# A last loop taken in halves: one PSUM bank for each z tile, a new order of steps, and batch ends stored late on two queues

## The chip, the cores and the metric

The kernel runs on one core of a Trainium2 chip. The core has five engines: PE (TensorE, matmuls; its weight loads are listed as PEld), DVE (VectorE), ACT (ScalarE), POOL (GpSimd) and SP (SyncE, which here only issues transfers), and 16 DMA engines that move data between the chip's memory and the core's. The metric is the device time of one launch in microseconds (us); smaller is better. A profile covers one execution, and its span is a little shorter than the time of the launch.

## The reference, cut to what matters

Attention with a causal mask and a decay bias makes `x`; a spectral layer follows. It transforms `x` over time, multiplies its 64 lowest modes by complex matrices (one 512 x 512 pair for each mode), transforms back to `y`, and returns `u + relu(u @ w_ch)` with `u = x + y`.

```python
# attention, for each of 8 batches and 8 heads, S = 576, D = 64
scores = where(causal, -1e9, scale * q @ k.T + minimum(bias, 0.0))
x = softmax(scores) @ v                       # -> (8, 576, 512)

# spectral layer
X = np.fft.rfft(x, axis=1)                    # only modes 0..63 are used
Y[:, :64] = X[:, :64] * (w_r + 1j * w_i)      # for each mode a 512x512 product
y = np.fft.irfft(Y, n=S, axis=1)
u = x + y
return (u + np.maximum(u @ w_ch, 0.0)).astype(np.float32)
```

The output is 8 x 576 x 512 float32, 9.44 MB. The weights `w_r` and `w_i` are 134 MB and are read once.

## The kernel before

The attention runs over 32 "images" (4 groups of two heads by 8 batches). While it runs, the weights of the modes are streamed in by transfers that POOL issues; the products of the modes follow as the weights come. The transform over time of one image:

```python
def fft(n):
    g, b = divmod(n, B)
    ps = auxpool.tile([P, 2, 3 * HM], FP32, name="ft_ps", tag="aux")     # HM = 32
    for T in range(NT):                                                  # NT = 5
        for q_ in range(2):
            nc.tensor.matmul(
                ps[HP * q_ : HP * q_ + HP].rearrange("p h f -> p (h f)"),
                x_all[:nT, g, b, T, q_::2], Ff_sb[:nT, T, :],            # 192 columns
                start=(T == 0), stop=(T == NT - 1), tile_position=(0, HP * q_), ...)
    for h in range(2):
        for q_ in range(2):
            ...                                                          # view a of ps
            nc.vector.tensor_copy(out=xs[g % 2][HP * h : HP * h + HP, q_, :, h, :, b, :], in_=a)
```

The output is made in 18 "pairs", each two tiles of 128 rows by 512 columns. A pair is two neighbouring tiles of one batch, or, twice, the ends of four batches: 576 = 4 x 128 + 64, so a batch's last 64 rows fill half a tile, and the ends of four batches fill one pair. The ends stand at places 2 and 4 of the list:

```python
pairs = [((b, T), (b, T + 1)) for b in range(B) for T in range(0, NF, 2)]   # NF = 4
for i, b in ((2, 0), (4, B // 2)):
    pairs.insert(i, ((b, NF), (b + 2, NF)))
NPRE = 2
kept = list(range(NPRE, len(pairs)))
ways = dict(zip(kept, "evgvggeggsgsgsgs"))
```

For a pair, `z = x @ w_ch + y @ w_ch`. The part from `x` is made earlier and kept in the core's memory (`z1s`, pairs 2 to 17); the letters say how it comes back: `e`, as two fp16 digits multiplied by the identity on PE; `s`, copied by ACT into the PSUM tile of z; `v`, added by DVE; `g`, added by POOL after ACT has copied z out. In the last loop each pair goes through these steps:

```python
zpool = ctx.enter_context(tc.tile_pool(name="z_psum", bufs=2, space=PSUM))   # a tile is two banks

def relu(i):                       # step R, ACT
    rs[i] = result(i)
    if ways.get(i) == "g":
        nc.scalar.copy(out=rs[i], in_=zs[i])
        nc.gpsimd.tensor_tensor(out=rs[i], in0=rs[i], in1=z1s[i], op=ALU.add)
        return
    n = 1 if i in (0, last) else 2
    for x in range(0, 2, n):
        nc.scalar.activation(out=rs[i][:, x : x + n], in_=zs[i][:, x : x + n], func=ACTF.Relu)
    if i in x_pool: ...            # x_pool is empty

def kept_sum(i):                   # step K, DVE
    rs[i] = result(i)
    nc.vector.tensor_tensor(out=rs[i], in0=zs[i], in1=z1s[i], op=ALU.add)

def finish(i):                     # step F, DVE and a store
    n = 1 if i in (0, last) else 2
    for x in range(0, 2, n):
        o, u = rs[i][:, x : x + n, :], us[i][:, x : x + n, :]
        if ways.get(i) in ("v", "g"):
            nc.vector.scalar_tensor_tensor(out=o, in0=o, scalar=0.0, in1=u, op0=ALU.max, op1=ALU.add)
        else:
            nc.vector.tensor_tensor(out=o, in0=u, in1=o, op=ALU.add)
        if T < NF:
            nc.sync.dma_start(out=out[b, ...].rearrange("(x p) e -> p x e", p=P), in_=o)
    if T == NF:
        for r, bb, _ in parts(b, T):                                     # two stores of 64 partitions
            nc.sync.dma_start(out=out[bb : bb + 3 : 2, NF * P :, :].rearrange("x t e -> t x e"), in_=rs[i][r])

steps = {"S": seed, "E": digits, "Z": add_z, "R": relu, "K": kept_sum, "X": add_x, "U": add_u, "F": finish}
for step in (
    "R0 X1 F0 U1 R1 E2 F1 Z2 Z3 R2 X2 K3 U2 Z4 F2 X3 R4 Z5 U3 K5 Z6 X4 R6 U4 F3 Z7 E8 R7 F4 Z8 X5 R8 "
    "Z9 U5 R9 X6 F5 U6 Z10 S11 F6 X7 U7 R10 Z11 F7 X8 R11 U8 Z12 F8 X9 S13 U9 X10 R12 F9 Z13 U10 R13 "
    "Z14 F10 X11 U11 S15 F11 X12 R14 U12 Z15 F12 X13 R15 U13 Z16 F13 X14 R16 U14 X15 F14 S17 U15 F15 "
    "X16 U16 Z17 F16 X17 R17 U17 F17 "
).split():
    steps[step[0]](int(step[1:]))
```

`Z` multiplies `y @ w_ch` (kept in `yv`) back over time into z, `X` puts `x` into the PSUM tile u, `U` adds `y` to it. Two matmuls of 512 columns make one such step of a full pair. `yv` is filled by small transfers (`spread`); the last of them comes after the last weights.

Of the kernel before, what the change touches and what calls it, by code (L numbers as in the profile page):

```python
# [18 lines left out]
def kernel(  # L19
# [60 lines left out]
    G_np = G_np.reshape(P, SP).astype(np.float16)  # L80
# [24 lines left out]
    G_sb = gp.tile([P, SP], FP16, name="G_sb")  # L105
# [318 lines left out]
    def fft(n):  # L424
        if n < 0:
            return
        g, b = divmod(n, B)
        ps = auxpool.tile([P, 2, 3 * HM], FP32, name="ft_ps", tag="aux")
        for T in range(NT):
            nT = tails[T]  # L430
            for q_ in range(2):
                nc.tensor.matmul(  # L432
                    ps[HP * q_ : HP * q_ + HP].rearrange("p h f -> p (h f)"),
                    x_all[:nT, g, b, T, q_::2], Ff_sb[:nT, T, :],
                    start=(T == 0), stop=(T == NT - 1),
                    tile_position=(0, HP * q_), skip_group_check=True,
                )
        for h in range(2):
            for q_ in range(2):
                a = ps[HP * q_ : HP * q_ + HP, h, : 2 * HM].rearrange("p (r m) -> p r m", r=2)  # L440
                a = bass.AP(tensor=a.tensor, offset=a.offset, ap=[a.ap[0], [HM, 2]] + list(a.ap[1:]))
                nc.vector.tensor_copy(out=xs[g % 2][HP * h : HP * h + HP, q_, :, h, :, b, :], in_=a)  # L442
# [50 lines left out]
    for i, b in ((2, 0), (4, B // 2)):  # L493
        pairs.insert(i, ((b, NF), (b + 2, NF)))
# [4 lines left out]
    ways = dict(zip(kept, "evgvggeggsgsgsgs"))  # L499
# [85 lines left out]
    zpool = ctx.enter_context(tc.tile_pool(name="z_psum", bufs=2, space=PSUM))  # L585
# [33 lines left out]

    def x_times_wch(i, last):  # L620
        zs[i] = z = zpool.tile([P, 2, DM], FP32, name="z_ps", tag="z")
        for x in range(2):
            for dt in range(DT):
                nc.tensor.matmul(  # L624
                    z[:, x, :], xts[i][:, x, dt, :], wch_sb[:, dt, :],
                    start=(dt == 0), stop=(last and dt == DT - 1), skip_group_check=True,
                )

    def keep(i):
        x_times_wch(i, True)  # L630
        j = late.index(i)
        if j < len(places):
            t = places[j]
        else:
            t = wpool.tile([P, WM, DM], BF16, name="z1", tag="w").rearrange("p m e -> p (m e)")
        kept_place(i, t)
        keep_product(i, slice(0, 2), zs.pop(i))
# [72 lines left out]
    x_pool = ()  # L710
    GK = P - 2 * MC * NX

    def add_y(dst, i, which, rows=slice(0, P), start=False):

        for x, (b, T) in enumerate(pairs[i]):
            for r, bb, _ in parts(b, T):
                nc.tensor.matmul(
                    dst[x][r, :], G_sb[rows, bass.ds(T * P, r.stop - r.start)],
                    yv[rows, bb, which, :], start=start, stop=True, skip_group_check=True,
                    tile_position=(0, r.start),  # L720
                )

    def add_last(dst, i, yb, cols=slice(0, DM), c=NX - 1):

        for x, (b, T) in enumerate(pairs[i]):
            nc.tensor.matmul(
                dst[x][:, cols], Gx_sb[:, c, bass.ts(T, P)], yb[:, cols],
                start=False, stop=True, skip_group_check=True,
            )
# [31 lines left out]
    def relu(i):  # L761

        rs[i] = result(i)
        if ways.get(i) == "g":
            nc.scalar.copy(out=rs[i], in_=zs[i])
            nc.gpsimd.tensor_tensor(out=rs[i], in0=rs[i], in1=z1s[i], op=ALU.add)  # L766
            return
        n = 1 if i in (0, last) else 2
        for x in range(0, 2, n):
            nc.scalar.activation(out=rs[i][:, x : x + n], in_=zs[i][:, x : x + n], func=ACTF.Relu)  # L770
        if i in x_pool:
            b, T = pairs[i][0]
            r = rs[i].rearrange("p x (g d) -> p x g d", d=P)
            nc.gpsimd.tensor_tensor(
                out=r, in0=r, in1=x_all[:, :, b, T : T + 2, :].rearrange("p g t d -> p t g d"), op=ALU.add
            )

    def kept_sum(i):
        rs[i] = result(i)
        nc.vector.tensor_tensor(out=rs[i], in0=zs[i], in1=z1s[i], op=ALU.add)  # L780

    def finish(i):
        n = 1 if i in (0, last) else 2
        b, T = pairs[i][0]
        for x in range(0, 2, n):
            o, u = rs[i][:, x : x + n, :], us[i][:, x : x + n, :]
            if ways.get(i) in ("v", "g"):
                nc.vector.scalar_tensor_tensor(out=o, in0=o, scalar=0.0, in1=u, op0=ALU.max, op1=ALU.add)
            else:
                nc.vector.tensor_tensor(out=o, in0=u, in1=o, op=ALU.add)  # L790
            if T < NF:
                nc.sync.dma_start(
                    out=out[b, bass.ds((T + x) * P, n * P), :].rearrange("(x p) e -> p x e", p=P), in_=o
                )
        if T == NF:
            for r, bb, _ in parts(b, T):
                nc.sync.dma_start(
                    out=out[bb : bb + 3 : 2, NF * P :, :].rearrange("x t e -> t x e"), in_=rs[i][r]
                )

    def z_of(i):
        return [zs[i][:, x, :] for x in range(2)]
# [55 lines left out]
    for i in range(NPRE):  # L858
        for cols in halves:
# [3 lines left out]
    def start_z(i):  # L863
        zs[i] = zpool.tile([P, 2, DM], FP32, name="z_ps", tag="z")

    def seed(i):
        start_z(i)
        nc.scalar.copy(out=zs[i], in_=z1s[i])

    def digits(i):  # L870
        start_z(i)
        for x in range(2):
            for y in range(2):
                nc.tensor.matmul(
                    zs[i][:, x, :], ident16h, z1s[i][:, y, x, :],
                    start=(y == 0), stop=False, skip_group_check=True,
                )

    def add_z(i):
        if i not in zs:  # L880
            start_z(i)
        add_y(z_of(i), i, 1, start=ways[i] in ("v", "g"))

    def add_u(i):
# [4 lines left out]

    steps = {  # L890
        "S": seed, "E": digits, "Z": add_z, "R": relu, "K": kept_sum, "X": add_x, "U": add_u, "F": finish,
    }
    for step in (
        "R0 X1 F0 U1 R1 E2 F1 Z2 Z3 R2 X2 K3 U2 Z4 F2 X3 R4 Z5 U3 K5 Z6 X4 R6 U4 F3 Z7 E8 R7 F4 Z8 X5 R8 "
        "Z9 U5 R9 X6 F5 U6 Z10 S11 F6 X7 U7 R10 Z11 F7 X8 R11 U8 Z12 F8 X9 S13 U9 X10 R12 F9 Z13 U10 R13 "
        "Z14 F10 X11 U11 S15 F11 X12 R14 U12 Z15 F12 X13 R15 U13 Z16 F13 X14 R16 U14 X15 F14 S17 U15 F15 "
        "X16 U16 Z17 F16 X17 R17 U17 F17 "
    ).split():
        steps[step[0]](int(step[1:]))
# [30 lines left out]
```

## Time and profile before

| | |
|---|---|
| time, median of 3 runs | 447.0 us (446.7 to 447.36) |
| span of the profiled execution | 445.1 us |
| busy: PE | 337.8 us (76%) |
| busy: DVE | 254.2 us (57%) |
| busy: ACT | 221.3 us (50%) |
| busy: POOL | 243.0 us (55%) |
| moved by the 16 DMA engines | 93.25 MB, mean 210 GB/s |

The busy shares are averages over stages with different limits, so none of them names the bound by itself. The page also cuts the span into 40 slices, follows the chain of work that ended last, and lists groups of instructions with their mean duration and the idle time before them. The trace answers the same by stretch of time. [...] Times within the span are counted from its start; the last loop begins at about 412.6 us.

### The profile page before, as it was taken

What the parts mean: (1) busy time and instruction counts of PE and PEld (TensorE: products, weight loads), DVE (VectorE), ACT (ScalarE), POOL (GpSimd) and SP (SyncE); (2) the same over time, 40 slices, a digit from 0 to 9 for tenths busy, and PEclk for the clock granted to TensorE, in tenths of its full rate; (3) what the DMA queues carried; (4) which work ended last, traced back from release to release, by engine and by line L of the source; (5) the groups of instructions that cost most, each with busy time, mean ns of one, the idle gap of its engine ahead of it and who ended that gap; (6) DMA issues with size and microseconds to landing.
All of it is one profiled execution on the core that took longest, in us unless ns stands there. A gap on an engine that the chain in (4) does not pass through costs nothing.

```text
span 445.1 us, 10791 instructions
## 1 busy us (share of the span) xinstructions
PE 337.8 (76%) x4409; PEld 209.9 (47%) x4409; DVE 254.2 (57%) x574; ACT 221.3 (50%) x387; POOL 243.0 (55%) x375
## 2 busy tenths in 40 slices
PE   1688897994908599792487859399987997768994
PEld 1365565563605465561354535266654555433341
DVE  7766776672705466662274627157765454541785
ACT  1576786463605374672263625267650344320593
POOL 7766666555556666455565546465544443530393
PEclk9998999996967889987598969689997799979998
DMA  9999999999999999999999999999999999996598
GB/s 174 202 206 205 204 207 204 207 207 208 207 209 202 205 203 187 207 206 209 207 200 206 209 206 203 208 205 205 199 209 211 210 210 210 209 218 131 168 351 346
DMA packets 72672, 93.25 MB, mean 210 GB/s; under 512 B 29664, under 2 KB 31200, under 8 KB 72624
## 3 DMA queue, kind: packets, MB, share of 16 engines
q0 software_dynamic: 63408, 81.29, 104.3%
q1 hardware_dynamic: 9216, 11.29, 7.9%
q8 instruction: 34, 0.56, 0.5%
q14 instruction: 14, 0.11, 0.1%
HBM read 163.51 MB, written 9.44 MB: 389 GB/s over the span
## 4 chain that ended last, share of the span: by engine, by line
DMA 58%; PE 22%; POOL 6%; issue 5%; DVE 5%; ACT 2%; POOLq 1%; DVEq 0%; ACTq 0%
DMA qk<-in_k_dram 19%; DMA w_sb<-in_moe_w_i_dram 16%; DMA w_sb<-in_moe_w_r_dram 16%; PE yp L452 4%; PE z_ps L624 4%; PE sc_ps L378 3%; POOL r_w L766 3%; PE tr_ps L336 2%; POOL w_sb L232 2%; PE sc_ps L372 2%; DMA x_all<-in_moe_w_r_dram 2%; DMA y_acc<-in_moe_w_r_dram 2%; DMA x_all<-in_moe_w_i_dram 2%; DMA v<-in_v_dram 1%; PE av_ps L407 1%
## 5 line engine op out<-in xcount | busy, mean ns | idle before, releaser
L386 ACT ACTIVATE p_sb<-sc_ps,cumt_sb 128x576 f16<-128x576 f32 (+1 forms) x256 | 141.9, 636 | 42.9 <-PE sc_ps L378 42.5
L232 POOL DMA_DIRECT2D w_sb<-in_moe_w_r_dram x120 | 71.2, 594 | 62.8 <-DMA w_sb<-in_moe_w_r_dram 16.7
L232 POOL DMA_DIRECT2D w_sb<-in_moe_w_i_dram x120 | 71.0, 594 | 61.0 <-DMA w_sb<-in_moe_w_i_dram 18.5
L340 DVE COPY qt<-tr_ps 64x576 bf16<-64x576 bf16 x64 | 47.8, 747 | 81.7 <-PE tr_ps L336 81.7
L336 PE MATMUL tr_ps<-ident,qk 64*64 64x64 bf16 x1152 | 35.4, 206 | 69.6 <-DMA qk<-in_k_dram 31.1
L378 PE MATMUL sc_ps<-qt,kt 128*128 128x512 bf16 (+2 forms) x384 | 77.8, 315 | 2.5 <-ACT kt L340 2.5
L232 POOL DMA_DIRECT2D v<-in_v_dram x72 | 52.1, 724 | 34.1 <-DMA w_sb<-in_moe_w_i_dram 8.8
L336 PEld LDWEIGHTS <-qk 64*64 64x64 bf16 x1152 | 26.9, 118 | 80.1 <-DMA qk<-in_k_dram 32.1
L372 PE MATMUL sc_ps<-negm,ident 128*128 128x256 bf16 x256 | 54.0, 296 | 0.2
L378 PEld LDWEIGHTS <-kt 128*128 128x128 bf16 x384 | 39.9, 106 | 27.5 <-issue 5.5
L357 ACT ACTIVATE p<-sc_ps,cumt 128x64 f16<-128x64 f32 x32 | 10.1, 314 | 78.9 <-PE sc_ps L353 78.9
L452 PE MATMUL yp<-w_sb,xs 128*32 128x512 bf16 (+1 forms) x480 | 39.0, 408 | 8.2 <-DMA w_sb<-in_moe_w_i_dram 2.3
L407 PE MATMUL av_ps<-v,p_sb 128*128 128x65 f16 x1024 | 43.0, 195 | 1.3 <-DVE x_all L417 0.6
L407 PEld LDWEIGHTS <-p_sb 128*128 128x128 f16 x1024 | 37.4, 98 | 7.5 <-DVE x_all L417 3.3
L442 DVE CAST xs<-ft_ps 64x128 bf16<-64x128 f32 x128 | 36.7, 287 | 2.9 <-PE ft_ps L432 1.2
L417 DVE TENSOR_TENSOR x_all<-av_ps,rcp 128x320 f16<-128x320 f32 x64 | 31.5, 492 | 2.2
L412 DVE TENSOR_REDUCE den<-av_ps 128x5 f32<-128x10 f32 x64 | 10.8, 169 | 37.9 <-PE av_ps L407 37.0
L340 ACT COPY kt<-tr_ps 64x576 bf16<-64x576 bf16 x32 | 23.0, 717 | 15.4 <-DVE qt L340 14.8
L452 PEld LDWEIGHTS <-xs 128*32 128x32 bf16 (+1 forms) x512 | 19.6, 143 | 22.8 <-issue 9.3
L624 PE MATMUL z_ps<-wch_sb,xs 128*128 128x512 f16 x96 | 25.3, 411 | 0.2 <-DVE xs L618 0.2
L432 PE MATMUL ft_ps<-Ff_sb,x_all 128*64 128x192 f16 (+1 forms) x320 | 24.4, 266 | 1.0 <-DVE x_all L417 1.0
L340 DVE COPY kt<-tr_ps 64x576 bf16<-64x576 bf16 x32 | 24.4, 763 | 0.4
(111 smaller groups left out, 416.0 us busy)
## 6 DMA issues: line engine op xcount, KB each, us to landing
w_sb<-in_moe_w_r_dram POOLq DMA_DIRECT2D x120, 256.0 KB, 8.7
w_sb<-in_moe_w_i_dram POOLq DMA_DIRECT2D x117, 256.0 KB, 8.7
out_dram<-r_w SPq DMA_DIRECT2D x14, 512.0 KB, 2.9
v<-in_v_dram POOLq DMA_DIRECT2D x72, 64.0 KB, 7.5
qk<-in_q_dram POOLq DMA_DIRECT2D x15, 288.0 KB, 7.9
qk<-in_k_dram POOLq DMA_DIRECT2D x15, 288.0 KB, 9.1
x_all<-in_moe_w_i_dram POOLq DMA_DIRECT2D x6, 256.0 KB, 7.6
out_dram<-r_w SPq DMA_DIRECT2D x6, 256.0 KB, 3.2
```

The source lines that it names most:

```text
L232: nc.gpsimd.dma_start(out=dst, in_=src)
L336: nc.tensor.transpose(ps[rows, r, :], src[rows, r, :], ident16[rows, rows])
L340: copy(out=to[:, :, :, half * RH : half * RH + RH], in_=ps[HP * i : HP * i + HP].rearrange("d r (h p) -> d h p r", h=2),)
L372: nc.tensor.matmul(ps[:, bass.ds(w * S, W)], ident16, negm[:, bass.ts(r, W)], start=True, stop=False, skip_group_check=True,)
L378: nc.tensor.matmul(ps[:, c0 : c0 + i1 - i0], keys[:, w, r, :], qh[:, i0:i1], start=False, stop=True, skip_group_check=True,)
L386: nc.scalar.activation(out=pt[:, poff[x] : poff[x] + S - w * W], in_=ps[:, w * S : (w + 1) * S - w * W], func=ACTF.Exp, bias=cumt_sb[:, x, ...
L407: nc.tensor.matmul(ps[:, I, r : r + NCH], lhsT, rhs, start=(i == 0), stop=(i == len(todo) - 1), skip_group_check=True,)
L417: nc.vector.tensor_tensor(out=x_all[:, g, b, :, D * h : D * h + D], in0=ps[:, :, 1 : NCH], in1=rcp.unsqueeze(2).to_broadcast([P, NT, D]), ...
L432: nc.tensor.matmul(ps[HP * q_ : HP * q_ + HP].rearrange("p h f -> p (h f)"), x_all[:nT, g, b, T, q_::2], Ff_sb[:nT, T, :], start=(T == 0), ...
L442: nc.vector.tensor_copy(out=xs[g % 2][HP * h : HP * h + HP, q_, :, h, :, b, :], in_=a)
L452: nc.tensor.matmul(ps[32 * cg : 32 * cg + 32, :], cols[k0:, q_, 1 - ri, :, c * MC // 2 + cg], wt[(g, c, ri, cg // 2)][k0:, 2 * (cg % 2) + ...
L624: nc.tensor.matmul(z[:, x, :], xts[i][:, x, dt, :], wch_sb[:, dt, :], start=(dt == 0), stop=(last and dt == DT - 1), skip_group_check=True,)
```

## The change

The change has these parts:

- The last loop works on half pairs. Each z tile is one PSUM bank of its own instead of a half of a two-bank tile, so that PE, ACT, DVE and POOL hand over halves (`a` and `b` in the list of steps). The number of banks for z stays four.
- The order of the steps was searched anew at that grain, and the ways of the kept products were chosen with it. POOL's addition is a step of its own (`G`).
- For pair 2, `x` isn't put into u by PE; POOL adds it to the result after the relu (`x_pool`).
- The batch ends stand at places 15 and 16, and their two stores are issued on two queues, SP's and ACT's (step `D`).
- The transform over time takes 96 columns a matmul instead of 192, with twice as many matmuls, and its evictions stay within their own partitions.
- The table of the inverse transform loses its padding (576 columns instead of 640), and the first two pairs' last products go by column halves first.

The aim is a last loop in which engines wait less for each other and the last stores go out sooner.

```diff
-    G_np = G_np.reshape(P, SP).astype(np.float16)
+    G_np = np.ascontiguousarray(G_np.reshape(P, SP)[:, :S].astype(np.float16))
...
-        for T in range(NT):
-            nT = tails[T]
-            for q_ in range(2):
-                nc.tensor.matmul(
-                    ps[HP * q_ : HP * q_ + HP].rearrange("p h f -> p (h f)"),
-                    x_all[:nT, g, b, T, q_::2], Ff_sb[:nT, T, :],
-                    ... tile_position=(0, HP * q_), ...
+        for q_ in range(2):
+            for T in range(NT):
+                nT = tails[T]
+                for h in range(2):
+                    nc.tensor.matmul(
+                        ps[HP * h : HP * h + HP, q_, :],
+                        x_all[:nT, g, b, T, q_::2],
+                        Ff_sb[:nT, T, 3 * HM * h : 3 * HM * (h + 1)],
+                        ... tile_position=(0, HP * h), ...
+                    )
+        for h in range(2):
+            rows = slice(HP * h, HP * h + HP)
+            for k in range(2):
+                nc.vector.tensor_copy(
+                    out=xs[g % 2][rows, :, k, h, :, b, :],
+                    in_=ps[rows, :, k * HM : (k + 2) * HM].rearrange("p q (r m) -> p q r m", r=2),
+                )
...
-    for i, b in ((2, 0), (4, B // 2)):
+    for i, b in ((15, 0), (16, B // 2)):
         pairs.insert(i, ((b, NF), (b + 2, NF)))
-    ways = dict(zip(kept, "evgvggeggsgsgsgs"))
+    ways = dict(zip(kept, "evgvegsggssgsgsg"))
...
-    zpool = ctx.enter_context(tc.tile_pool(name="z_psum", bufs=2, space=PSUM))
+    zpool = ctx.enter_context(tc.tile_pool(name="z_psum", bufs=1, space=PSUM))
+    def start_z(i, x):
+        zs[i, x] = zpool.tile([P, DM], FP32, name="z_ps", tag=f"z{i % 2}{x}")
...
-        keep_product(i, slice(0, 2), zs.pop(i))
+        for x in range(2):
+            keep_product(i, x, zs.pop((i, x)))
...
-    x_pool = ()
+    x_pool = (2,)
...
+    def relu(i, x):
+        if i not in rs:
+            rs[i] = result(i)
         if ways.get(i) == "g":
+            nc.scalar.copy(out=rs[i][:, x], in_=zs[i, x])
+        else:
+            nc.scalar.activation(out=rs[i][:, x], in_=zs[i, x], func=ACTF.Relu)
+
+    def gpsimd_sum(i, x):
+        r = rs[i][:, x]
+        if ways.get(i) == "g":
+            nc.gpsimd.tensor_tensor(out=r, in0=r, in1=z1s[i][:, x], op=ALU.add)
+        else:
+            ... nc.gpsimd.tensor_tensor(out=r, in0=r, in1=x_all[:, :, b, T, :], op=ALU.add)
...
+    def finish(i, x=None):
...
         if T == NF:
+            store_tails(nc.sync, i, 0)
...
+    def store_tails(queue, i, y):
+        r, bb, _ = parts(b, T)[y]
+        queue.dma_start(out=out[bb : bb + 3 : 2, NF * P :, :].rearrange("x t e -> t x e"), in_=rs[i][r])
...
-    for i in range(NPRE):
-        for cols in halves:
+    for cols in halves:
+        for i in range(NPRE):
             add_last(z_of(i), i, vb, cols)
...
+        "F": finish, "D": lambda i: store_tails(nc.scalar, i, 1),
...
+        "R0a X1 R0b U1 F0a R1a E2a F0b E2b R1b U2 F1 Z2a Z2b R2a Z3a Z3b K3a X3 R2b G2a Z4a K3b U3 R4a Z4b "
+        "F3 Z5a G2b R4b E6a Z6a E6b R6a K5a G4a Z6b Z5b S8a X5 F2 Z7a R6b U5 G4b R7a Z8a K5b X4 S8b U4 F5 "
+        "R8a G7a Z7b Z9a R7b Z10a Z8b F4 R9a X7 G7b U7 R8b Z9b S11a Z10b G9a X6 F7 R9b U6 R10a Z11a S11b "
+        "G9b F6 X9 S12a U9 R11a Z11b G10a Z12a F9 R10b X8 U8 R12a Z13a G10b S12b F8 X11 R11b U11 R13a Z12b "
+        "Z13b F11 X10 R12b G13a U10 R13b Z15a S14a F10 X13 G13b R15a Z15b Z14a S14b U13 Z17a R15b G15a F13 "
+        "X12 R17a U12 R14a Z17b G15b Z14b F12 R17b X15 S16a U15 G17a R14b X14 F15 Z16a S16b U14 R16a G17b "
+        "Z16b F14 X17 D15 R16b U17 F17a X16 F17b U16 F16 D16 "
```

## The prediction

> **What bounds the kernel now.** I read the page's slices and its chain first, to see which stage the change can reach. The first row gives the busy share of the 16 DMA engines in 40 slices of 11.1 us, the second what they moved, the last line the chain by engine.
>
> ```profile
> DMA  9999999999999999999999999999999999996598
> GB/s 174 202 206 205 204 207 204 207 207 208 207 209 202 205 203 187 207 206 209 207 200 206 209 206 203 208 205 205 199 209 211 210 210 210 209 218 131 168 351 346
> DMA 58%; PE 22%; POOL 6%; issue 5%; DVE 5%; ACT 2%; POOLq 1%; DVEq 0%; ACTq 0%
> ```
>
> For 36 slices the loads run at some 205 GB/s with the engines full, and 58% of the chain is DMA. In order of time the chain leaves that stage with the last weight load and then passes through one small transfer:
>
> ```profile
> 398.07 10.43 DMA w_sb<-in_moe_w_i_dram
> 408.55 0.67 PE yp L452 x4
> ...
> 412.13 3.22 DMA yv<-v_sb
> 415.39 1.16 PE z_ps L717 x6
> ```
>
> So up to 408.5 us the transfers set the time, and up to 415.4 us a short dependent path that the change barely touches. Only the last loop, 415.4 to 445.1, has something to give. Its stretches, with busy us of PE, PEld, DVE, ACT and POOL, then clock, DMA share and GB/s:
>
> ```profile
> 415.00:424.00 9.00, 8.61 (x49) 3.14 (x50) 6.79 (x6) 5.18 (x6) 4.78 (x3) 1.00 0.68 233
> 424.00:432.00 8.00, 7.80 (x35) 3.30 (x34) 7.11 (x6) 7.47 (x8) 8.00 (x4) 1.00 0.99 353
> 432.00:441.00 9.00, 6.96 (x30) 2.82 (x29) 8.48 (x9) 5.31 (x7) 5.93 (x3) 1.00 1.02 395
> 419.00:420.00 1.00, 1.00 (x7) 0.33 (x6) 0.91 (x1) 0.18 (x2) 0.78 (x1) 1.00 0.00 0
> 421.00:422.00 1.00, 1.00 (x7) 0.45 (x6) 0.83 (x2) 0.41 (x1) 1.00 (x2) 1.00 0.96 223
> 428.00:430.00 2.00, 1.93 (x9) 0.78 (x8) 1.93 (x2) 1.97 (x3) 2.00 (x2) 1.00 1.05 410
> 443.00:444.00 1.00, 0.00 (x0) 0.00 (x0) 0.00 (x0) 0.00 (x0) 0.00 (x0) 0.50 0.39 148
> ```
>
> No engine stands out: DVE is 94% busy at the end, POOL full in the middle, and the DMA engines are full from 421 on. A pair's result is 512 KB, 1.28 us at the 410 GB/s of 428 to 430. The batch ends (pairs 2 and 4 here) leave as two stores of 64 partitions, and the second of 421 to 422, when only they were under way, moved 223 GB/s at a share of 0.96: 2.35 us for 512 KB, 1.07 more. Stores of pairs 2 to 17 thus need 14 x 1.28 + 2 x 2.35 = 22.6 us. The first byte of pair 2 moves at about 420.4 (nothing in the second from 419; 0.62 of the next is busy), the last at about 443.4 (0.39 of the second from 443). That is 23.0 us. The store stream has hardly a gap, so it is the real bound of this loop, and DVE's speed matters by when it starts the stream and whether it keeps it fed.
>
> The kinds of instruction that the change touches (count, busy us, mean ns, idle before):
>
> ```profile
> L788 DVE SCALAR_TENSOR_TENSOR r_w<-r_w,u_ps 128x1024 f32<-128x1024 f32 x10 | 12.1, 1219 | 2.5 <-PE u_ps L717 1.3 <-POOL r_w L766 0.9
> L765 ACT COPY r_w<-z_ps 128x1024 f32<-128x1024 f32 x8 | 8.1, 1011 | 2.7 <-PE z_ps L717 2.7
> L770 ACT ACTIVATE r_w<-z_ps 128x512 f32<-128x512 f32 x2 | 1.1, 594 | 1.8 <-issue 1.8
> L790 DVE TENSOR_TENSOR r_w<-u_ps,r_w 128x512 f32<-128x512 f32 x2 | 1.3, 682 | 0.0
> L766 POOL TENSOR_TENSOR r_w<-r_w,z 128x1024 f32<-128x1024 f32 x6 | 14.0, 2356 | 0.1
> ```
>
> [...] an ACT half takes 594 ns and a full one 1011, though two halves in a row took 1.09 us together.
>
> **The change part by part.**
>
> *Transform over time.* For each of 32 images, 10 matmuls of 192 columns become 20 of 96. Ten now pass in 0.66 us (62.64 to the next group at 63.30). A full matmul of 512 columns starts every 0.215 us, 0.42 ns a column, so 96 columns need up to 40 ns; the 64x64 transposes show that 22 ns apiece can be had (18 in 0.40 us). Twenty: 0.44 to 0.80 us, so -0.2 to +0.1 us an image, up to 5 us of PE in all. The four evictions of 287 ns keep their number and size. PE waits often in this stage (the idle time of the transposes alone, for k, is 31.1 us), and DMA is full. On the path: 0, at most +0.5.
>
> *Kept products in halves.* Ten copies of 1.01 us become ten pairs of about 1.09: +0.8 us of ACT between 340 and 400 us, where ACT is busy less than half the time. On the path: 0.
>
> *The batch ends at places 15 and 16.* The first store after 415.4 is now a full pair. PE: two z matmuls of pair 2, then two of pair 3, from 415.39, each 0.215 apart; the first z half of pair 3 is done by about 416.2. DVE adds its two halves (1.28 us), then finishes pair 3 (1.14, the distance of two finishes in a row): 418.65 at best. Pair 2 was finished at 418.98. A store's first byte moves about 1.1 us after its DVE result (pair 0: its first half is done at 413.89, and the engines are full from 415.0), so the stream starts at about 419.8 instead of 420.4: 0.6 us gained. In the new order two half sums of pair 5 stand between the next finishes, so the stores of pairs 2 and 5 start near 421.6 and 423.2, with gaps of 0.85 us in the stream before it is saturated: 0.85 lost. From there DVE needs 1.14 a pair and a store 1.28, so the stream stays the bound.
>
> *Two queues for the batch ends.* If both halves run together at the full rate, 2 x 1.07 = 2.1 us are saved; if as now, nothing. At place 15 the second half is issued from ACT after a few more instructions, beside a full store from the other queue, so at least some overlap is likely. I count half: 1.1 gained.
>
> *The end.* Before, the last half of pair 17 was finished at 440.88 and its 256 KB were the last bytes. Now 512 KB of pair 16 follow the last finish; since the stream is behind DVE anyway, this costs only where DVE is late. I allow 0.3.
>
> *Work on the engines after 415.4.* PE: pair 2's x leaves (2 x 0.215 = 0.4). ACT: 17 full (0.96 apart) and two halves are 17.4 us; 38 halves at about 0.5 are 19.0, and two store issues come on top: +2.8, in a window of 22. POOL: 16 halves for 8 full, 18.7 us or somewhat more, the first at about 416.4 instead of 419.22. DVE: 15 x 1.14 + 3 x 1.28 = 20.9 us, as before (20.7), of which it waited 3.6 (416.59 to 440.88 is 24.3). For the stream it may wait about 1.8 without harm: DVE could be done at 437.2 and is needed by 439.0.
>
> Sum: -0.6 + 0.85 - 1.1 + 0.3 = -0.55 us; 0.45 more for smaller waits of DVE on PE and POOL (1.3 and 0.9 above), which the halves and POOL's early start should cut. Together -1.0: 446.0 us, with a span near 444.1.
>
> **The rivals.** *Everything fits:* both halves of a batch end at full rate and DVE never late. Then the stream ends at 419.8 + 20.5 + 0.85 = 441.1 instead of 443.4, and the time is 444.7. For it: all engines have their work 1 to 3 us inside the window. *The half-rate stores move to where the stream is full and nothing hides them:* [...] the stream ends at 441.1 + 2.1 = 443.2, plus the end's 0.3 or more, and the time is 447.0 to 447.5. For it: in the trace a batch end alone kept the engines at 0.96 and moved half. *ACT becomes the bound:* 21 us of 22, one bank a tile, each half waiting for PE and PE for it. Each us that pair 16's relu comes late is one on the end: 447.5 to 448. Against it: ACT had 2.7 us of waits on z in eight copies, and finer pieces shorten just those. *The transform's extra matmuls and weight loads delay loads:* +0.5, hardly more, since the DMA engines are full for 36 slices.
>
> **Range and chances.** Best of the rivals 444.7, worst 448; in the middle 446.0, and the three runs before lie within 0.7 us. I take 444.6 to 447.4. For 2%, 8.9 us, the loop would have to shrink from 29.7 to 20.8 us, hardly more than the 20.5 us of stores alone; for 2% slower something in the load stage must break. So faster 0.01, slower 0.01, same 0.98.
>
> **What would show it.** Right: the first full store at about 419 us, the batch ends' stores above 300 GB/s where they overlap, DVE's waits after 415.4 near 2 us, the last byte near 442.3, and weights still ending at 408.5. Wrong: seconds of 220 GB/s at a full share near the end (half rate unhidden), ACT without gaps while DVE waits on it, or the weight stage ending elsewhere than within 0.5 us of 408.5.

## The result and the profile after

The changed kernel took 449.39 us (median of 6 runs, 447.9 to 450.48) against 446.74 us for the kernel before beside it: a ratio of 1.0056, 95% interval 1.0035 to 1.0076. Repeated later with 22 runs it gave 448.91 us against 446.97, a ratio of 1.0037 (1.0025 to 1.0049). So it is slower by about 0.4%, 1.6 to 2.5 us. Predicted were 446.0 us, 444.6 to 447.4.

The slices of the changed kernel's page, in the same rows as before:

```profile
DMA  9999999999999999999999999999999999994697
GB/s 175 201 207 205 203 202 205 207 205 208 206 209 200 204 206 182 208 207 208 206 203 206 209 207 202 209 206 204 208 210 210 209 210 209 209 214 88 241 365 250
DMA 51%; PE 30%; DVE 7%; POOL 5%; issue 3%; ACT 1%; DVEq 0%; POOLq 0%; ACTq 0%
```

The load stage looks as it did: 36 full slices near 205 GB/s. The last slice moves 250 GB/s where it had moved 346. In order of time (start, length, what), the end of the changed kernel's chain:

```profile
397.87 11.94 DMA w_sb<-in_moe_w_i_dram
409.86 0.67 PE yp L456 x4
413.44 3.02 DMA yv<-v_sb
...
437.18 1.22 DVE r_w L803
438.44 0.62 PE u_ps L756 x4
439.06 0.57 PE u_ps L727 x4
439.76 1.18 DVE r_w L803
```

Two things are to be seen. The last weights were used at 409.86 instead of 408.55. That is scatter and not the change: the last weight packet ended at 409.5 here, in a second profile of the same kernel (e13 below) at 407.6, and in the experiments, whatever their transform, between 407.5 and 409.0 us. And the chain of waits stops at DVE's last finish, 440.94, though the span is 448.2. The rest is 7.3 us: 5.7 until the last byte of the stores, 1.6 from there to the end of the span. In the kernel before (last finish 440.88, span 445.1) it was 2.6 and 1.6. The trace says what became of the stores. Windows of the changed kernel, with the columns of the prediction's table:

```profile
415.00:424.00 9.00, 8.79 (x41) 3.71 (x39) 8.33 (x11) 7.24 (x14) 6.25 (x6) 1.00 0.64 240
424.00:432.00 8.00, 7.94 (x38) 3.17 (x36) 7.57 (x7) 8.00 (x18) 7.75 (x7) 1.00 0.90 332
432.00:439.00 7.00, 6.93 (x38) 2.18 (x36) 5.73 (x6) 5.56 (x11) 5.61 (x5) 1.00 1.03 378
439.00:446.00 7.00, 0.62 (x6) 0.13 (x4) 1.94 (x3) 0.00 (x0) 0.00 (x0) 0.67 0.97 290
428.00:430.00 2.00, 2.00 (x10) 0.87 (x9) 2.00 (x3) 2.00 (x5) 1.92 (x2) 1.00 1.02 371
439.00:440.00 1.00, 0.62 (x6) 0.13 (x4) 1.00 (x3) 0.00 (x0) 0.00 (x0) 1.00 0.99 225
```

The engines did what the change was for. DVE was busy 8.33 us of the first nine instead of 6.79. The gate is here the small transfer of `yv` in the chain, for which the z matmuls of the last loop wait; from the first z matmul after the gate (416.51) to its last finish it took 24.4 us instead of 25.5. But the DMA engines, full at 1.02 in 428 to 430, moved 371 GB/s where the kernel before moved 410, and no batch end was being stored then. From 439 on they were full at 290 GB/s, down to 225: there the batch ends go out. So there are two losses in the stores, one of which the prediction had not named at all.

The packets in the trace show the first loss more finely. All stores consist of packets of 2048 bytes (4608 of them from 415 us on, the whole output). Between 428 and 434 us:

```
                            packets  mean ns   at most 85 ns   86 ns or more
the kernel before           1140     84.0      100%            0%
the changed kernel          1018     88.3      64%             36%
```

### The profile page after: what moved, and what is told of

It is laid out like the page before. It is cut to its first block, busy times and chain, and to the rows that moved or that the text cites. A ratio compares the mean times of both kernels' runs of the same rounds, so it can differ in the third digit from the quotient of the medians.

```text
span 448.2 us, 11468 instructions
## 1 busy us (share of the span) xinstructions
PE 348.2 (78%) x4727; PEld 220.1 (49%) x4727; DVE 251.6 (56%) x577; ACT 224.5 (50%) x417; POOL 244.0 (54%) x383
## 4 chain that ended last, share of the span: by engine, by line
DMA 51%; PE 30%; DVE 7%; POOL 5%; issue 3%; ACT 1%; DVEq 0%; POOLq 0%; ACTq 0%
DMA w_sb<-in_moe_w_i_dram 17%; DMA qk<-in_k_dram 16%; DMA w_sb<-in_moe_w_r_dram 11%; PE yp L456 5%; PE sc_ps L378 5%; PE av_ps L407 4%; PE ft_ps L433 4%; PE sc_ps L372 3%; PE tr_ps L336 3%; POOL w_sb L232 2%; DMA x_all<-in_moe_w_r_dram 2%; DMA y_acc<-in_moe_w_r_dram 2%; DMA x_all<-in_moe_w_i_dram 2%; DVE kt L340 1%; PE z_ps L631 1%
## 5 line engine op out<-in xcount | busy, mean ns | idle before, releaser
L456 PE MATMUL yp<-w_sb,xs 128*32 128x512 bf16 (+1 forms) x480 | 40.0, 416 | 8.5 <-DMA w_sb<-in_moe_w_i_dram 2.4
L407 PE MATMUL av_ps<-v,p_sb 128*128 128x65 f16 x1024 | 44.3, 198 | 0.1
L407 PEld LDWEIGHTS <-p_sb 128*128 128x128 f16 x1024 | 38.6, 100 | 4.7 <-DVE x_all L417 1.6
L443 DVE CAST xs<-ft_ps 64x128 bf16<-64x128 f32 x128 | 31.4, 284 | 8.3 <-PE ft_ps L433 7.5
L433 PE MATMUL ft_ps<-Ff_sb,x_all 128*64 128x96 f16 (+1 forms) x640 | 33.5, 226 | 1.0 <-DVE x_all L417 1.0
L433 PEld LDWEIGHTS <-x_all 128*64 128x64 f16 (+1 forms) x640 | 22.8, 115 | 9.1 <-DVE x_all L417 1.1
```

The source lines that it names most:

```text
L407: nc.tensor.matmul(ps[:, I, r : r + NCH], lhsT, rhs, start=(i == 0), stop=(i == len(todo) - 1), skip_group_check=True,)
L433: nc.tensor.matmul(ps[HP * h : HP * h + HP, q_, :], x_all[:nT, g, b, T, q_::2], Ff_sb[:nT, T, 3 * HM * h : 3 * HM * (h + 1)], start=(T == ...
L443: nc.vector.tensor_copy(out=xs[g % 2][rows, :, k, h, :, b, :], in_=ps[rows, :, k * HM : (k + 2) * HM].rearrange("p q (r m) -> p q r m", r=2),)
L456: nc.tensor.matmul(ps[32 * cg : 32 * cg + 32, :], cols[k0:, q_, 1 - ri, :, c * MC // 2 + cg], wt[(g, c, ri, cg // 2)][k0:, 2 * (cg % 2) + ...
```

## The experiments

A ratio is always that to the kernel before, run on the same chip beside it; its interval is given in brackets. "Last byte" is the end of the last store packet.

**First runs: the transform, the second queue, the batch ends' stores.** The first edit puts the transform of 192 columns back into the changed kernel; the second puts the transform of 96 columns into the kernel before; both use the code shown in the change. The third and fourth:

```diff
 # e3: the four stores of the batch ends are left out (1 MB of the output is not written)
     def store_tails(queue, i, y):
-        ... queue.dma_start(out=out[bb : bb + 3 : 2, NF * P :, :]..., in_=rs[i][r])
+        pass
 # e4: both halves from SP
-            store_tails(nc.sync, i, 0)
+            for y in range(2):
+                store_tails(nc.sync, i, y)
-        "D": lambda i: store_tails(nc.scalar, i, 1),
+        "D": lambda i: None,
```

> The changed kernel with the transform of 192 columns put back. If the transform of 96 columns is what delays the last weights (409.86 us in the changed kernel against 408.55 before), they end near 408.5 again and the time falls from 449.4 to about 448.2. If the whole loss is in the stores of the last loop, the time stays within 0.4 us of 449.4.

> The kernel before with only the transform changed to 96 columns. If the transform costs something, 447.9 or so, and runs that scatter as those of the changed kernel do (447.9 to 450.5); if it is free, 446.5 to 447.2 as before.

> The changed kernel without the four stores of the batch ends (1 MB of the output is not written). If these stores run at half rate at the end with nothing to hide them, they are worth 2 x 2.35 us of the stream and the time falls by 4 to 5 us, to about 445. If they overlap with other stores at the full rate, they are worth 2 x 1.28 us, and the time falls by 2.6 us or less.

> The changed kernel with both halves of a batch end issued from SP right after its finish, none from ACT. If two queues help (halves together at the full rate), it becomes slower by 1 to 2 us. If the halves share the same engines whatever the queue, it stays within 0.4 us, or gains a little because ACT no longer holds its relus back while it issues.

Measured: e1 447.85 us, 1.0020 (1.0007 to 1.0034); e2 447.46, 1.0014 (1.0003 to 1.0024); e3 444.41, 0.9945 (0.9933 to 0.9958); e4 448.34, 1.0028 (1.0017 to 1.0039).

e3 is clear. Without the batch ends' stores the changed kernel is 4.5 to 5 us faster than with them, whichever of its two medians is taken, while at the 410 GB/s of the kernel before their 1 MB would be 2.6 us of stream, an estimate. They run below that rate (290 GB/s from 439 on) with nothing to hide them. e4 answers the two queues: with one queue the kernel is not slower, as it would be if two ran the halves together at the full rate. The trace of the changed kernel shows why nothing was gained on the first batch end. Both halves were issued at the same moment:

```profile
437.01 0.69 SPq L815 DMA_DIRECT2D out_dram<-r_w  x1
437.01 0.73 ACTq L815 DMA_DIRECT2D out_dram<-r_w  x1
```

But the packets of ACT's half moved only from 439.93 to 442.05, when those of SP's half were nearly through: the halves followed one another, and ACT's then ran in part beside the next full store.

e1 and e4 looked like gains of 1.5 and 1.0 us over the changed kernel's 449.4. The repeat of the changed kernel (e13, below) took most of that back: against 1.0037 all the intervals overlap. What e2 shows holds: the transform alone costs 0.1 to 1.1 us, most likely about 0.5. A transform in the timeline of PE, in the kernel before and then in the changed one:

```profile
62.64 0.73 PE L432 MATMUL ft_ps<-Ff_sb,x_all 128*64 128x192 f16 x10
```

```profile
62.16 0.98 PE L433 MATMUL ft_ps<-Ff_sb,x_all 128*64 128x96 f16 x20
```

Over the 32 images (medians) the starts lie on average 51 ns apart for 192 columns and 39.5 ns for 96 (one matmul is listed with 246 and 207 ns, so the records overlap and the distance of the starts counts). So a transform takes 0.75 instead of 0.46 us from its first start to its last: 0.29 us more an image, 9.4 us of PE in all, of which e2's time shows about 0.5.

**Second runs: order of addresses, place of the batch ends.** All four have the transform of 192 columns and one queue.

```diff
 # e6, e8: neighbours among the full pairs exchanged, so that the steps, which finish
 #         3, 2, 5, 4, 7, 6, ..., write the output in order of address
+    for i in range(2, 14, 2):                    # e8: range(6, 18, 2)
+        pairs[i], pairs[i + 1] = pairs[i + 1], pairs[i]
 # e7, e8: batch ends at the places that are finished first and third after the gate
-    for i, b in ((15, 0), (16, B // 2)):
+    for i, b in ((3, 0), (5, B // 2)):
```

> The changed kernel with the transform of 192 columns and with both halves of a batch end issued from SP. If the two costs found (0.9 to 1.5 us of transform, 1.0 to 1.3 of the second queue) are separate, they add up: 449.4 - 2.5 = 446.9, level with the kernel before. If both were the same delay, 447.8 or more.

> As the run before, and with the neighbours of places 2 to 13 exchanged, so that the same steps write the output in order of address (the changed order finishes 3, 2, 5, 4, 7, 6). If the order of addresses is why its stores run at some 375 GB/s between 426 and 438 us instead of 405, the rate returns to 400 or more and the time falls by 0.5 to 1 us. If not, no difference over 0.3 us.

> As the first run of this call, with the batch ends at places 3 and 5, the first and third to be finished, instead of 15 and 16. If the half-rate stores cost because nothing hides them at the end, they now fall into the gaps at the start of the stream, and the time falls by 1 to 2 us, to 445 to 446. If the end is bound by DVE and not by the stores, no difference over 0.4 us.

> Both together: batch ends at places 3 and 5 and stores in order of address. If both theories hold, the fastest of all, 444.5 to 445.5; if only that of the half-rate stores holds, level with the run before.

Measured: e5 448.31 us, 1.0033 (1.0023 to 1.0043); e6 448.20, 1.0026 (1.0016 to 1.0035); e7 448.42, 1.0029 (1.0016 to 1.0043); e8 448.49, 1.0036 (1.0025 to 1.0047). All level. Two theories fell here: storing the output in order of address brought nothing that shows (e6 against e5, e8 against e7), and neither did moving the batch ends to the front alone (e7 against e5). e5 didn't add up the gains that e1 and e4 had seemed to show. In e7 the packets still took 87.1 ns on average between 428 and 434, and only 68% of them at most 85, with no batch end under way. So the slow packets come neither from the transform, nor from the second queue, nor from the places. They are also there in the changed kernel's first stores (86.6 ns on average between 415 and 418 us, 84.0 in the kernel before), before there is much for halves to disturb. That pointed to something fixed: where the tiles lie.

**Third runs: the address.** The table of the inverse transform lost its padding, 640 to 576 columns of 2 bytes. The compiled programs' list of addresses shows what follows: every tile allocated after it moved by 128 bytes. The result tiles stood at 97792, 101888, ... bytes of a partition, multiples of 256 and of 512 alike, and now stand at 97664, 101760, ..., which are 128 lower. No run tries another offset, so which multiple counts, if any, is not shown. e9 cuts the table as the change does; e10 pads only the tile in the core's memory and leaves the constant in the chip's memory cut, so it tests the tiles' addresses alone.

```diff
 # e9: the kernel before, with the table cut as in the change, nothing else
-    G_np = G_np.reshape(P, SP).astype(np.float16)
+    G_np = np.ascontiguousarray(G_np.reshape(P, SP)[:, :S].astype(np.float16))
-    G_sb = gp.tile([P, SP], FP16, name="G_sb")
+    G_sb = gp.tile([P, S], FP16, name="G_sb")
 # e10: the changed kernel, with the tile's 128 bytes back and unused
-    G_sb = gp.tile([P, S], FP16, name="G_sb")
+    G_sb = gp.tile([P, SP], FP16, name="G_sb")
-    nc.sync.dma_start(out=G_sb, in_=d_G)
+    nc.sync.dma_start(out=G_sb[:, :S], in_=d_G)
 # e11: e5 and e12: e7, each with e10's edit
```

> The kernel before with only the table of the inverse transform cut from 640 to 576 columns, which moves every later tile of the core's memory by 128 bytes: the result tiles then start 128 bytes off a multiple of 256. If that is why the changed kernel's store packets take 86 to 88 ns and more instead of 84, its packets do too, the stream runs at some 380 GB/s and the time rises by about 1 us to 448. If the slow packets come from the half pairs or the order of steps, packets stay at 84 ns and the time at 447.0.

> The changed kernel with the table's tile back at 640 columns (64 unused), nothing else. By the theory of the address: packets of 84 ns outside the batch ends, 400 GB/s or more between 426 and 438 us, and about 1 us less than the changed kernel: 448.2 or below. By the theory of the half pairs: packets and time as in the changed kernel.

> Padded table, transform of 192 columns, both halves of a batch end from SP. By the theory of the address 1 us less than the same without the padding (448.3): 447.3, level with the kernel before, because the half-rate stores still stand at the end.

> As the run before, with the batch ends at places 3 and 5. With full-rate packets the place of the half-rate stores should now show: 446 to 446.5, faster than the kernel before. If the place makes no difference, as it made none without the padding, 447.3.

Measured: e9 448.05 us, 1.0029 (1.0017 to 1.0040); e10 447.86, 1.0024 (1.0015 to 1.0034); e11 447.95, 1.0026 (1.0015 to 1.0036); e12 446.96, 1.0001 (0.9987 to 1.0016).

e9 is the cleanest run of the study. Counted from the gate, every instruction of its last loop starts within 0.02 us of where it did, and it lost 1.2 us. The same two windows of the kernel before, then of e9:

```profile
433.00:438.00 5.00, 4.66 (x21) 1.95 (x20) 4.82 (x5) 3.23 (x4) 4.50 (x3) 1.00 1.04 402
438.00:443.00 5.00, 1.48 (x7) 0.49 (x5) 2.67 (x4) 1.09 (x2) 0.43 (x1) 0.94 1.05 407
```

```profile
433.00:438.00 5.00, 4.65 (x22) 1.94 (x20) 4.82 (x5) 3.24 (x4) 4.50 (x3) 1.00 1.02 381
438.00:443.00 5.00, 1.50 (x7) 0.49 (x5) 2.68 (x4) 1.09 (x2) 0.45 (x1) 1.00 1.02 379
```

The engines' columns are the same to a few hundredths; only the last one fell, from 402 and 407 GB/s to 381 and 379. Packets between 428 and 434 us:

```
                                            mean ns   at most 85 ns
the kernel before                           84.0      100%
e9,  the kernel before, table cut           87.5       73%
the changed kernel, second profile (e13)    87.4       68%
e10, the changed kernel, table padded       84.1       99%
e12, padded, ends at places 3 and 5         84.2       98%
```

The address is shown in both directions: 87.5 ns a packet in e9, where the tiles moved, and 84.1 in e10, where they moved back. In e9 packets took 4% longer on average than in the kernel before and the rate fell by 5 to 7%. Why is not shown: 73% of the packets took at most 85 ns, as before, and the others up to 133.

e10 then shows the second loss alone, windows near the end of the loop:

```profile
433.00:435.00 2.00, 2.00 (x12) 0.47 (x10) 1.74 (x2) 1.97 (x5) 2.00 (x3) 1.00 0.91 352
436.00:438.00 2.00, 1.66 (x11) 0.38 (x8) 1.92 (x4) 0.55 (x1) 0.00 (x0) 1.00 0.76 175
438.00:443.00 5.00, 0.00 (x0) 0.00 (x0) 1.04 (x1) 0.00 (x0) 0.00 (x0) 0.91 0.99 333
```

In 433 to 435 the stream waits for work: the share is 0.91. In 436 to 438 the first half of a batch end is almost alone and moves 175 GB/s at a share of 0.76, and in the last five microseconds of full engines (438 to 443) the ends' stores pull the mean to 333. The last byte comes 4.7 us after DVE's last finish (439.04, 443.71). In e12, where the batch ends are stored first, the end of the loop is clean and they stand at 421:

```profile
421.00:422.00 1.00, 1.00 (x8) 0.35 (x8) 0.73 (x2) 0.95 (x2) 0.29 (x2) 1.00 0.95 205
...
433.00:438.00 5.00, 4.66 (x21) 1.92 (x20) 4.83 (x5) 4.20 (x9) 4.58 (x4) 1.00 1.05 408
438.00:443.00 5.00, 0.72 (x4) 0.11 (x2) 2.04 (x3) 0.00 (x0) 0.00 (x0) 0.87 1.03 400
```

Here the last byte comes 3.6 us after the last finish.

The packets tell the two stores of a batch end apart. The first takes partitions 0 to 63, the second 64 to 127, 128 packets each (here in the order of their starts):

```
                              first store              second store
                              median ns  start to end  median ns  start to end
the kernel before, at 420.35  153        1.54 us       84         0.86 us
the kernel before, at 424.12  153        1.52          84         0.85
e12, at 420.39                153        1.55          84         1.02
e11, at 437.59                153        1.55          84         1.12
```

Only the first store of a batch end is slow in these traces, at 420, 424 and 437 us alike; on ACT's queue, beside stores of SP, the second's median is 84 ns too, its mean 129 (e10). Both together take 2.2 us in the kernel before, 0.9 more than a full pair. The second of 421 to 422, from which the prediction took half rate for both, straddles the two. No run separates the partitions from the order of the stores and the rows they write, so why only one is slow stays open.

The table of the two causes, with the ratios to the kernel before:

```
                          ends at 15 and 16              ends at 3 and 5
tiles 128 bytes off       1.0037 (e13), 1.0033 (e5)      1.0029 (e7), 1.0036 (e8)
tiles in their old places 1.0024 (e10), 1.0026 (e11)     1.0001 (e12), 1.0007 (e14)
```

Against the changed kernel either remedy alone brings some 0.1%, no more than an interval is wide, and both together 0.3%. A second measure, one trace of each kernel, leaves the scatter of the load stage out: the time from the first z matmul after the gate to the last byte, in us. Kernels with the same last loop agree in it within 0.4.

```
                            two queues,         one queue,          one queue,
                            ends at 15 and 16   ends at 15 and 16   ends at 3 and 5
tiles 128 bytes off         30.2, 30.0, 29.9    29.5, 29.2, 29.0    29.3, 29.3
                            (changed, e13, e1)  (e4, e5, e6)        (e7, e8)
tiles in their old places   29.1 (e10)          29.1 (e11)          28.4, 28.5 (e12, e14)

the kernel before 28.1; with the transform of 96 columns (e2) 28.5;
with the table cut (e9) 29.1; with its ends at 15 and 16 (e15) 30.4
```

With one queue the two causes stand side by side as two limits: against e5 the address alone brings 0.1 us (e11), the place alone nothing (e7), both 0.8 (e12). In these runs the stream ends when its bytes are through, and, where the last finish is a batch end's, not before some 4.7 us after it. In e5 and e11 DVE's last finish comes 24.4 us after the gate, and the last byte 4.8 and 4.7 us later, whatever the address; in e7 and e12, where a full pair is last, it comes after 24.9 us in both, and the last byte 4.4 and 3.6 us later. It also explains why e5 to e8 are level. With two queues the address alone brings 0.9 us (30.0 to 29.1). That a second queue costs 0.5 us or more when the tiles are off would fit these traces, but not the times (e1 1.0020, e5 1.0033), and stays open.

**Fourth runs: what was left open.** e13 is the changed kernel unaltered. The others:

```diff
 # e14: e12 with the transform of 96 columns
 # e15: the kernel before, only the places of the batch ends
-    for i, b in ((2, 0), (4, B // 2)):
+    for i, b in ((15, 0), (16, B // 2)):
 # e16: e12, pair 2 finished first, in halves, with x from PE
-    x_pool = (2,)
+    x_pool = ()
-        "... R1b U2 F1 Z2a Z2b R2a Z3a Z3b K3a X3 R2b G2a Z4a K3b U3 R4a Z4b F3 Z5a G2b R4b ... S8a X5 F2 Z7a ..."
+        "... R1b F1 Z2a Z2b R2a X2 U2 Z3a Z3b R2b F2a K3a X3 F2b Z4a K3b U3 R4a Z4b F3 Z5a R4b ... S8a X5 Z7a ..."
```

> The changed kernel once more, unaltered. If the first six runs were typical, 1.0056 of the kernel before (449.4). If the transform and the second queue cost little, as the runs with the padded table say, 1.003 to 1.004: some 448.3.

> The changed kernel with padded table and batch ends at places 3 and 5 on one queue, but with the transform of 96 columns kept. If that transform is free, level with the same with 192 columns (1.0001 of before); if it costs what the first call suggested, 1.002 to 1.003.

> The kernel before with its batch ends at places 15 and 16 instead of 2 and 4, nothing else. By the theory of the half-rate stores about 1 to 2 us slower (1.002 to 1.004), though its last store stays a half pair of 256 KB. If the place doesn't matter, 1.000.

> The kernel of batch ends at places 3 and 5 with padded table and 192 columns, in which pair 2 gets its x from PE and is finished first, in halves, before the sums of pair 3. If the end follows the start of the store stream, it gains the part of 2 us by which the first store after the gate comes earlier: 0.5 to 1.2 us, 445.7 to 446.4, faster than both kernels. If the end is bound elsewhere, 447.0.

Measured: e13 448.91 us, 1.0037 (1.0025 to 1.0049); e14 447.48, 1.0007 (0.9993 to 1.0021); e15 449.27, 1.0045 (1.0027 to 1.0064); e16 448.56, 1.0033 (1.0021 to 1.0045).

e13 corrects the reading of e1 and e4, as told above. e14 is not distinguishable from e12, nor from e2's cost for the transform. e15 confirms the place of the batch ends in the old loop, with its tiles in their old places and nothing else edited (the pairs between move by one or two places): 2 us slower. Windows of e15:

```profile
428.00:430.00 2.00, 1.93 (x10) 0.81 (x9) 1.93 (x2) 1.92 (x2) 2.00 (x2) 1.00 1.05 409
...
440.00:442.00 2.00, 0.54 (x3) 0.05 (x1) 1.75 (x3) 0.85 (x2) 0.00 (x0) 1.00 0.82 193
```

e16 was meant to beat both kernels and missed. Its first store after the gate did start earlier (418.6 instead of 420.4), but then the stream starved. The same three windows of e12, then of e16:

```profile
416.00:420.00 4.00, 4.00 (x24) 1.20 (x20) 3.50 (x5) 2.62 (x6) 3.73 (x4) 1.00 0.35 137
420.00:428.00 8.00, 7.84 (x40) 3.15 (x39) 6.70 (x7) 7.54 (x16) 6.62 (x6) 1.00 0.92 282
428.00:443.00 15.00, 10.38 (x46) 4.24 (x44) 11.47 (x11) 9.20 (x19) 9.32 (x8) 0.96 1.04 404
```

```profile
416.00:420.00 4.00, 4.00 (x23) 1.19 (x22) 2.85 (x6) 2.21 (x4) 0.88 (x1) 1.00 0.61 235
420.00:428.00 8.00, 7.84 (x39) 3.03 (x38) 6.34 (x7) 7.09 (x14) 6.01 (x6) 1.00 0.64 173
428.00:443.00 15.00, 11.60 (x52) 4.75 (x49) 12.58 (x12) 10.42 (x21) 10.53 (x9) 1.00 1.05 404
```

From 428 on both run at 404 GB/s. Up to 420 e16 was 0.4 MB ahead (235 against 137 GB/s); in the eight us after that it moved 173 GB/s against 282, 0.9 MB less. The balance, 0.5 MB, is worth 1.2 us at 404, of the 1.6 by which it is slower than e12. What counts here is not the first byte but the time from which the stream has no gap. No version tried here is faster than the kernel before; e12 and e14 are level with it.

## Why the prediction was wrong, point by point

**The bound was read rightly.** The load stage, the gate and the store stream behaved as said. e9 shows the stream as the bound: slower packets alone, with no engine later, cost 1.2 us.

**The step that failed outright was one that isn't in it.** The change's list had the table that loses its padding. The prediction gave it no part and no cost: it looked like 16 KB less to load. It moved every later tile by 128 bytes, the result tiles too, and took 5 to 7% of the stream's rate ("a store 1.28" became about 1.37 at 382 GB/s). In the kernel before it costs 1.2 us alone (e9), in the changed kernel 0.6 by the times (e13 and e10) and 0.9 by the traces. The prediction took 410 GB/s for granted in its sums, and "all engines have their work 1 to 3 us inside the window" couldn't see it, for it isn't work of an engine.

**"I count half: 1.1 gained" for the two queues was wrong.** Two queues gained nothing that shows: padded, 1.0024 with two and 1.0026 with one (e10, e11, which also differ in the transform), and 29.1 us from gate to last byte in both. The halves of the first batch end, issued together, ran one after the other. The half was my estimate, from a hope of overlap that no run had shown. There was also less to gain: the half rate, read from 223 GB/s against 410 and taken for both stores, holds only for the one from partitions 0 to 63 (153 ns a packet); the one from 64 to 127 was not slow (84 ns), and a batch end takes 0.9 us more than a full pair, not 1.07. Where a batch end and full stores ran together the rate was between: 290 GB/s from 439 to 446, under the 300 that the prediction named as its sign of being right.

**"The end" was mis-sized: 0.3 allowed.** With batch ends last, the last byte comes 4.7 us after the last finish (e10) instead of 2.6 in the kernel before (440.88 to 443.48) and 3.6 in e12. And "DVE could be done at 437.2 and is needed by 439.0", that is 21.8 and 23.6 us after the gate, did not hold: it was done 24.4 us after it. With full-rate packets the place of the ends is worth 0.7 (traces) to 1.0 us (times) in the new loop (e10 and e11 against e12) and 2 us in the old one (e15). This is the second rival of the prediction, "the half-rate stores move to where the stream is full and nothing hides them". It was set at 447.0 to 447.5; with the address repaired the run that isolates it gave 447.9 (e10).

**The stream's early start held.** "0.6 us gained": from the first z matmul after the gate to the first byte of the next store it took 4.4 us instead of 5.0 (416.51 to 420.91, 415.39 to 420.35), and DVE was done 1.1 us sooner after the gate. "0.85 lost" in gaps before the stream is full held too: 0.80 in two gaps (422.34 to 422.64, 424.06 to 424.56). The "0.45 more for smaller waits" came true on DVE, whose listed waits after the gate fell from 3.0 to 1.9 us, but not in the time, for the stream ends after DVE. The searched steps did what they were searched for. The gain was spent in the stores.

**ACT was not the bound.** It was busy all of 424 to 432 (8.00 of 8), as that rival had it, but DVE waited on it for only 0.4 us after the gate. The groups of the changed kernel:

```profile
L801 DVE SCALAR_TENSOR_TENSOR r_w<-r_w,u_ps 128x1024 f32<-128x1024 f32 x8 | 9.7, 1220 | 1.7 <-PE u_ps L727 0.7 <-issue 0.3 <-POOL r_w L785 0.2
L785 POOL TENSOR_TENSOR r_w<-r_w,z 128x512 f32<-128x512 f32 x8 | 10.0, 1271 | 0.4 <-ACT r_w L777 0.3
```

DVE's waits before these finishes fell from 2.5 us (ten) to 1.7 (eight), and the part due to POOL from 0.9 to 0.2. A half on POOL takes 1271 ns, 8% over half of the 2356 of a full one.

**The transform:** "-0.2 to +0.1 us an image" was wrong, it is +0.29. Twenty at 39.5 ns take 0.79 us, inside the 0.44 to 0.80 allowed, though far from the 22 ns that the prediction read from the transposes; the base was wrong. Ten starts 51 ns apart take 0.51 us, and the 0.66 that I read as ten matmuls held 0.15 of passing on to the next group. "On the path: 0, at most +0.5" was about met: e2's most likely value lies at that edge, its interval reaches 1.1.

**The sum.** From the gate to the last byte the kernel before takes 28.1 us, and the prediction took 1.0 off. e10, the change without the moved address, takes 29.1, so 1.0 more. Of this the early start is -0.6 and the first gaps, here 0.97, are +1.0; what is left, +0.6 by subtraction, stands where the prediction had -1.1 for the queues, +0.3 for the end and -0.45 for DVE's waits. The address adds 0.9 to 1.1 (30.0 and 30.2 in the two traces of the changed kernel). So two steps failed, the batch ends' stores last and on two queues, and the missing term for the address; either alone is enough to miss the 1.0 us. Nor does the gain appear with both repaired: e12 is level with the kernel before. Its batch ends come first again, and its stream starts 5.2 us after the gate, so the early start is lost with them; e16, which starts it at 3.1, starves it.

## What to carry to other kernels

Stores were the bound here, and moving the tiles they leave from by 128 bytes cost the kernel before 1.2 us (e9: 87.5 ns a packet against 84.0); unused padding took the packets back to 84.1 (e10). So look at what a changed allocation does to all tiles after it. A slow store, here the first half of each batch end (153 ns a packet against 84), did better where the stream has gaps, at the start of the output stage, than at its end (e12 446.96 us against 447.95 in e11; e15 2 us slower than the kernel before), and a second queue didn't mend it (e10, e11). When two limits stand side by side, undoing either alone can show next to nothing (here, from the gate to the last byte and against e5, 0.1 us in e11, nothing in e7, both together 0.8 in e12); try the remedies together before dropping a theory.

## What the runs showed of the hardware that I hadn't expected

A store packet of 2048 bytes took 84.0 ns on average, none over 85, from the result tiles of the kernel before, and mostly 84 ns, in a quarter of cases up to 133, 87.5 on average, from the same tiles 128 bytes lower (e9, both from 428 to 434 us); with all 16 engines busy that was 402 to 407 GB/s against some 380. Of a batch end's two stores of 64 partitions, the first had packets of 153 ns (median), the second of 84, in the kernel before, e11 and e12 alike. While the first was under way the engines' share was near 1 (0.95 at 209 GB/s in the second from 437 in e10): a full share didn't say that the engines moved what they can. The load stage, whose weight tiles moved by the same 128 bytes, kept its rate and its end: its packets of 2048 bytes took 173.7 ns in e9 and 173.6 in the kernel before, and the last ended at 408.1 and 408.2 us.
